# Two transformer layers on one core: late query projections split between two memories, epsilon on GpSimd, and a planner that books transfers and a slow clock

## The chip, the cores and the metric

One core of one Trainium2 chip. The time is that of the device in microseconds for one execution, from first to last instruction and what lies around them; lower is better. The engines are TensorE (PE in the profile; its weight loads are PEld), VectorE (DVE), ScalarE (ACT), GpSimd (POOL) and SyncE (SP), which issues nearly all transfers. Scores, projections and attention sums are made by TensorE in PSUM, in banks of 512 float32 columns.

## The reference

Two layers, each an attention part and a dense part with a squared ReLU, over 2048 tokens of 448 features; 16 heads of 28 features, 1792 hidden features, one set of weights for both layers, bfloat16.

```python
def _A_ref(x, wqkv, wo):
    H = 16; Dh = D // H
    q, k, v = ...
    p = _softmax(jnp.einsum("bhqd,bhkd->bhqk", q, k) * Dh ** -0.5, axis=-1)
    o = jnp.einsum("bhqk,bhkd->bhqd", p, v)
    return ... @ wo
def _B_ref(x, w1, b1, w2, b2):
    h = jnp.maximum(x @ w1 + b1, 0)
    return (h * h) @ w2 + b2
x = A_x
for layer in range(2):
    x = x + _A_ref(_layernorm(x), A_wqkv, A_wo)
    x = x + _B_ref(_layernorm(x), B_w1, B_b1, B_w2, B_b2)
return x
```

The layer norm is (x - mean) / sqrt(variance + 1e-5) over the features.

## The kernel before

**Work.** Tokens stand in 16 tiles of 128. Heads stand in four groups g of four, each head in a band of 32 rows or columns. Queries go in blocks of 256 (the last two of layer 1 in blocks of 128). For a layer, a query block and a group of heads there is a pass: over all keys, scores are made (`sc`, L1326), exponentials taken (`pt`), and the products with the values summed in one bank (`oT`, L1516). A unit is 512 columns of scores, one bank; there are 2048 units.

**Exponentials on two engines.** A turn of `s_stream` makes three or four units. ScalarE takes two or three banks with one instruction (L1369). The remaining unit, if `apart` allows it, goes to VectorE: a taking (L1389) writes a piecewise linear power of two as int16, two shifted copies follow (L1405, on GpSimd or VectorE, whichever the planner finds sooner), and VectorE adds one of the copies to the first line (L1418). Memory that is dead at the time serves for them, in cells of 512 columns that `cells` lists: nine of its own (`v_c`), and parts of the keys and values of the layer that isn't running, of `K_sb[0]` among them.

**Rows after attention.** VectorE copies or adds the sums out of PSUM (L1539, L1541). The softmax sums stand in one row of each band; `norm_pair` sends them through transfers: spread out (`dn`), inverted by VectorE (L1621), written to DRAM (`scr`) and brought back to all rows of a band (`rec`), then multiplied (L1640). For the last blocks `norm_turn` inverts them on VectorE alone, with two transposes and no transfer (L1582 to L1598). `chain` then makes the output projection, the layer norm, the hidden layer with ReLU (L1720) and square (L1727), the second matrix, and in layer 0 the next layer's projections of the block (`qkv`).

**Layer norm.** VectorE takes mean and variance (L672, L677), adds epsilon (L700), GpSimd raises to the power -1/2 (L697, `rstd`), VectorE normalizes (L796).

**Late queries.** In layer 0, while block qb runs, layer 1's normalized input of blocks 4 to 7 is stored in `Q_sb` at the block's own columns, since its queries can only be written when layer 0's are dead. The projections for these blocks (`late_queries`) are then made in two halves, of two groups each. Both read all of the stored input and write over it; so the copy of the first half waits, through the token `qq`, until the matmuls of the second are done.

**Beside other work.** A projection of K = 4 x 128 rows leaves its last 128 rows to guests: `visit` makes it in bands of 32 rows beside score matmuls that use other bands (L927); what found no place is made whole at the end (`fin`, L870). Score matmuls are repeated as filler, and junk matmuls (`heat`) made, where the recent load of TensorE is low.

**The order.** The program is built by `Planner.run`: generators offer operations, each with an engine, a booked duration and what it depends on; the planner picks the one that can start first (with priorities) and issues it, so each engine's row is fixed beforehand. Its numbers are set again and again while it runs: `PACE` maps the count of exponentials so far to values for the names of the rules, and `FORCE` and `SKIP` name turns in which a unit must or mustn't go to VectorE. Transfers are an engine of the planner too, "DMA": `dur` is the time for which a transfer keeps that engine, `lat` what passes after it until the data is there.

Of the kernel before, what the change touches and what calls it, by code (L numbers as in the profile page):

```python
# [29 lines left out]
def lines(x, by):  # L30
# [138 lines left out]
GNEXT = 0.5  # L169
BEHIND = 3  # L170
# [9 lines left out]
         'GUEST': 1, 'GUEST1': 0, 'GUESTB': 1, 'STEER': 1, 'GWAIT': 1, 'GOPEN': 0.8},  # L180
    8: {'EV': 3.5, 'FORCE': (15,)},
    16: {'LOW': 0.5, 'SKIP': (18,)},
    24: {'EPRIO': 6, 'MARGIN': 3, 'FORCE': (29,)},
    32: {'ASIDE': 0, 'V_PRIO': 3},
    40: {'RES2': 4},
    48: {'HOLD': 5, 'SKIP': (49,)},
    56: {'EV': 2.9},
    64: {'MMC': 0.46, 'SKIP': (71,)},
    72: {'TASIDE2': -0.2, 'V_LAST': 2.5},
    80: {'MMC': 0.3, 'LEAD': 6, 'GNEXT': 0.3},  # L190
    88: {'MMC': 0.46, 'BUSY': 0.95, 'PRE': 1.2},
    104: {'TB2': 2.4, 'SOON': 1},
    120: {'LAG': 12, 'V_PRIO': 6},
    128: {'TASIDE2': -0.4, 'GOPEN': 2, 'SPAN': 15},
    144: {'MORE': 1, 'ASIDE': 0.2, 'FORCE': (148,)},
    160: {'HEAT': 0.45, 'V_LATE': 4.6},
    168: {'PORTP': 0.1, 'SKIP': (171,)},
    176: {'PNEAR': 0.35, 'FORCE': (181,)},
    192: {'V_AGE': 8, 'SKIP': (198,)},
    224: {'MFREE': 1, 'GIDLE': 0.1, 'FORCE': (226,)},  # L200
    256: {'V_PAST': 3},
    264: {'C_PRIO': 2.6, 'V_PRIO': 3, 'SKIP': (271,)},
    272: {'LADD': 0.1, 'BEHIND': 0, 'PMAX': 6},
    280: {'NEAR_U': 6},
    288: {'LAG': 1, 'SOON': 1.5, 'C_PRIO': 2.1, 'SKIP': (295,)},
    296: {'GIDLE': 0.5},
    312: {'V_PRIO': 6},
    320: {'BUSY': 1.0},
    328: {'EPRIO': 4, 'GIDLE': 0.1, 'SKIP': (332,)},
    336: {'PLIM': 4, 'LADD': 0.3},  # L210
    344: {'PORTP': 0.3, 'SKIP': (348,)},
    360: {'V_AGE': 6, 'PORTP': 2, 'C_PRIO': 1.6},
    368: {'LADD': 0.05, 'FORCE': (369,)},
    384: {'PORTP': 0.3},
    392: {'MFREE': 5, 'KEEP': 3, 'PWAIT': 1.5, 'SKIP': (393,)},
    408: {'SOON': 0.3, 'FORCE': (413,)},
    416: {'SPARE': 0},
    432: {'SPARE': 3, 'PORTP': 2, 'SKIP': (439,)},
    440: {'LAG': 16},
    448: {'URGE': 8, 'ASIDE': 2},  # L220
    456: {'PRE': 0.3},
    464: {'LADD': 0, 'PWAIT': 0.6},
    472: {'V_AGE': 8, 'SKIP': (479,)},
    480: {'V_WAIT': 8},
    488: {'LAG': 3},
    496: {'BUSY': 1.05, 'CHUNK': 2},
    512: {'PWAIT': 0.1, 'V_PAST': 1},
    520: {'RES': 1},
    536: {'TB2': 1.6, 'FAR': 9, 'MORE': 3, 'FORCE': (537,)},
    544: {'V_WAIT': 3, 'NEAR_U': 0},  # L230
    560: {'RES2': 2, 'SKIP': (563,)},
    568: {'RES': 4},
    576: {'EV': 3.5, 'SKIP': (583,)},
    584: {'LEAD': 2},
    592: {'SKIP': (599,)},
    600: {'PWAIT': 0.3},
    608: {'HEAT': 0.3},
    616: {'HEAT': 0.45, 'V_LAST': 3},
    624: {'VGAP': 0.08},
    632: {'BEHIND': 3, 'URGE': 3, 'BUSY': 1.0},  # L240
    640: {'MFREE': 1},
    648: {'V_PAST': 2, 'SKIP': (649,)},
    656: {'V_LAST': 2.2, 'PRE': 0, 'SKIP': (658,)},
# [36 lines left out]
class Planner:  # L280
# [3 lines left out]
    def __init__(self):  # L284
# [11 lines left out]
        self.seen = []  # L296

# [43 lines left out]
    def run(self):  # L341
        while self.streams:
# [88 lines left out]
def kernel(  # L431
# [77 lines left out]
    def flat_of(t):  # L509
        return t[:, :, :].rearrange("p g s -> p (g s)")  # L510
# [1321 lines left out]
```

## Time and profile before

| | |
|---|---|
| median of 3 runs (802.45 to 804.76) | 804.6 us |
| the profiled execution | 803.5 us |
| its span, first to last instruction | 801.7 us |
| first exponential starts, last one ends | 9.16 us, 786.60 us |
| mean granted TensorE clock | 0.994 |
| moved by transfers | 18.12 MB, mean 23 GB/s |

The page of a profile gives for each engine its busy time and its share of the span. A table of stages gives the same for stretches of the span, and the granted clock in each. A line on a group of instructions names the line of the program, the engine, the operation, what is written from what, its shapes and count, then the busy time and the mean duration of one in ns, then the engine's idle time just before them and what ended most of it. A group's busy time is less than count times mean where neighbours on an engine overlap.

### The profile page before, as it was taken

What the parts mean: (1) busy time and instruction counts of PE and PEld (TensorE: products, weight loads), DVE (VectorE), ACT (ScalarE), POOL (GpSimd) and SP (SyncE); (2) the same over time, 40 slices, a digit from 0 to 9 for tenths busy, and PEclk for the clock granted to TensorE, in tenths of its full rate; (3) what the DMA queues carried; (4) which work ended last, traced back from release to release, by engine and by line L of the source; (5) the groups of instructions that cost most, each with busy time, mean ns of one, the idle gap of its engine ahead of it and who ended that gap; (6) DMA issues with size and microseconds to landing.
All of it is one profiled execution on the core that took longest, in us unless ns stands there. A gap on an engine that the chain in (4) does not pass through costs nothing.

```text
span 801.7 us, 29097 instructions
## 1 busy us (share of the span) xinstructions
PE 769.9 (96%) x12227; PEld 412.2 (51%) x12227; DVE 736.9 (92%) x1645; ACT 783.8 (98%) x701; POOL 439.9 (55%) x677
## 2 busy tenths in 40 slices
PE   9999988999999999999999999889999999999997
PEld 6455544555535455454545445435455455445665
DVE  8999998999999999999999999889999999999854
ACT  9999999999999999999999999999999999999994
POOL 3266664565675575465455566545666566675200
PEclk9999999999999999999999999989999999999999
DMA  9300011000000000000000000011000000000000
GB/s 248 87 3 2 3 30 30 16 17 16 7 12 16 16 17 16 16 3 16 2 2 3 2 2 3 6 38 32 23 21 22 27 22 23 21 18 13 21 21 13
DMA packets 32479, 18.12 MB, mean 23 GB/s; under 512 B 17818, under 2 KB 31899, under 8 KB 32348
## 3 DMA queue, kind: packets, MB, share of 16 engines
q1 hardware_dynamic: 32204, 16.16, 7.3%
q8 instruction: 95, 1.56, 0.8%
q14 instruction: 36, 0.29, 0.1%
q10 hardware_dynamic: 144, 0.11, 0.0%
HBM read 13.98 MB, written 2.06 MB: 20 GB/s over the span
## 4 chain that ended last, share of the span: by engine, by line
PE 65%; ACT 18%; DVE 11%; issue 5%; DMA 2%; POOL 0%; ACTq 0%; SPq 0%; DVEq 0%
PE mt L851 27%; PE sc L1326 18%; ACT pt L1369 18%; PE oT L1516 14%; PE mt L927 2%; DVE pt L1389 2%; PE tp L736 1%; PE sc L851 1%; DVE st L672 1%; DVE x_sb L1649 1%; DVE v_c L1389 1%; DMA scr<-dn 1%; DVE xn L796 1%; DVE Q_sb L945 1%; PE mt L870 1%
## 5 line engine op out<-in xcount | busy, mean ns | idle before, releaser
L1369 ACT ACTIVATE pt<-sc 128x1536 bf16<-128x1536 f32 (+1 forms) x683 | 771.9, 1285 | 5.6 <-PE sc L1326 4.9
L1326 PE MATMUL sc<-Q_sb,K_sb 32*128 32x256 bf16 (+1 forms) x4562 | 277.4, 266 | 17.9 <-ACT pt L1369 14.6
L1516 PE MATMUL oT<-pt,V_sb 128*32 128x256 bf16 (+1 forms) x4062 | 191.0, 269 | 2.0 <-DVE Q_sb L945 0.8
L1326 PEld LDWEIGHTS <-K_sb 32*128 32x128 bf16 x4562 | 98.9, 92 | 167.1 <-issue 111.0
L1389 DVE TENSOR_SCALAR pt<-sc 128x512 int16<-128x512 f32 x207 | 141.0, 683 | 9.9 <-PE sc L1326 8.6
L1516 PEld LDWEIGHTS <-V_sb 128*32 128x32 bf16 x5074 | 117.2, 96 | 61.2 <-issue 56.3
L1405 POOL TENSOR_SCALAR v_c<-pt 128x512 int16<-128x512 int16 x160 | 107.5, 672 | 64.8 <-DVE pt L1389 27.3
L851 PE MATMUL mt<-xnT,w 128*128 128x256 bf16 (+1 forms) x912 | 120.6, 270 | 1.5 <-DVE r L1720 1.2
L1405 POOL TENSOR_SCALAR K_sb<-pt 128x512 int16<-128x512 int16 x114 | 75.7, 664 | 48.5 <-DVE pt L1389 23.5
L851 PEld LDWEIGHTS <-w 128*128 128x128 bf16 x952 | 78.4, 98 | 36.6 <-issue 28.1
L1720 DVE TENSOR_SCALAR r<-mt 128x512 bf16<-128x512 f32 x107 | 72.9, 683 | 7.4 <-PE mt L851 7.1
L1516 PE MATMUL oT<-v_c,V_sb 128*32 128x256 bf16 (+1 forms) x436 | 65.4, 276 | 1.9 <-DVE r L1720 1.4
L851 PE MATMUL mt<-w,V_sb 128*128 128x448 bf16 x274 | 65.3, 355 | 0.0
L697 POOL TENSOR_TENSOR rstd<-mv,mhalf 128x2 f32<-128x2 f32 (+1 forms) x34 | 24.7, 727 | 65.1 <-DVE mv L700 46.2
L1405 POOL TENSOR_SCALAR V_sb<-pt 128x512 int16<-128x512 int16 x66 | 42.9, 650 | 24.9 <-DVE pt L1389 11.7
L1418 DVE TENSOR_TENSOR pt<-pt,v_c 128x512 bf16<-128x512 bf16 x96 | 41.2, 435 | 2.4 <-POOL v_c L1405 2.0
L1405 POOL TENSOR_SCALAR v_c<-v_c 128x512 int16<-128x512 int16 x47 | 31.0, 660 | 21.4 <-DVE v_c L1389 12.4
L1516 PE MATMUL oT<-K_sb,V_sb 128*32 128x256 bf16 (+1 forms) x304 | 42.4, 269 | 0.1
L1649 DVE TENSOR_TENSOR x_sb<-x_sb,mt 128x448 bf16<-128x448 bf16 x61 | 37.1, 610 | 3.1 <-PE mt L851 2.6
L672 DVE BATCH_NORM_STATS2 st<-x_sb 128x6 f32<-128x448 bf16 x63 | 38.6, 614 | 0.5 <-DMA x_sb<-in_A_x_dram 0.4
L1389 DVE TENSOR_SCALAR v_c<-sc 128x512 int16<-128x512 f32 x55 | 37.5, 681 | 1.5 <-PE sc L1326 1.4
L1405 POOL TENSOR_SCALAR V_sb<-V_sb 128x512 int16<-128x512 int16 x40 | 26.5, 662 | 21.2 <-DVE V_sb L1389 10.4
(172 smaller groups left out, 1031.7 us busy)
## 6 DMA issues: line engine op xcount, KB each, us to landing
rec<-scr SPq DMA_DIRECT2D x54, 128.0 KB
out_dram<-x_sb SPq DMA_DIRECT2D x15, 112.0 KB
x_sb<-in_A_x_dram SPq DMA_DIRECT2D x7, 224.0 KB
w<-in_B_w_dram SPq DMA_DIRECT2D x1, 1568.0 KB
w<-in_B_w_dram SPq DMA_DIRECT2D x1, 1344.0 KB
dn<-oT_sb SPq DMA_DIRECT2D x54, 4.0 KB
V_sb<-in_A_wqkv_dram SPq DMA_DIRECT2D x4, 168.0 KB
scr<-dn SPq DMA_DIRECT2D x27, 8.0 KB
```

The source lines that it names most:

```text
L672: nc.vector.bn_stats(out=box["st"][:, :], in_=x_sb[:, t0 + j, :] if src is None else src())
L697: nc.gpsimd.tensor_tensor(out=rstd[:, a:b], in0=mv[0][:, a:b, 1], in1=mhalf[:, a:b], op=ALU.pow)
L851: nc.tensor.matmul(box["t"][:, c0:c0 + n], lhsT=lhsT() if callable(lhsT) else lhsT, rhs=rhs, start=a and "x" not in rest, stop=b or stop is m)
L927: t = nc.tensor.matmul(rest["box"]["t"][:, c0:c0 + n], lhsT=lhsT[rows], rhs=rhs[rows], start=start and j == 0, stop=stop and j == len(rest ...
L1326: nc.tensor.matmul(dst[k][:, i * nt * P:(i + 1) * nt * P], lhsT=K_sb[l][rows, g, (kb + i) * P:(kb + i + 1) * P], rhs=Q_sb[rows, g, t0 * P: ...
L1369: t = nc.scalar.activation(out=pt[:, 0:n], in_=gbuf[gi]["sc"][:, 0:n], func=AF.Exp, scale=float(np.log(2.0)) * 2.0 ** -FRAC)
L1389: t = nc.vector.tensor_scalar(out=z.bitcast(DT.int16), in0=src, scalar1=EXP_BASE, scalar2=0.0, op0=ALU.add, op1=ALU.max)
L1405: (nc.vector if e == "DVE" else nc.gpsimd).tensor_scalar(out=box[k].bitcast(DT.int16), in0=gbuf[gi]["z"].bitcast(DT.int16), scalar1=1.0, s ...
L1418: nc.vector.tensor_tensor(out=z, in0=z, in1=box[1], op=ALU.add)
L1516: nc.tensor.matmul(box["t"][DHP * hh:DHP * hh + DHP, 0:n], lhsT=V_sb[l][:, tb, 4 * g + hh, :], rhs=p, start=hh in starts and j == begins[h ...
L1649: nc.vector.tensor_tensor(out=x_sb[:, tb, lo:hi], in0=x_sb[:, tb, lo:hi] if src is None else src[:, lo:hi], in1=t[:, 0:hi - lo], op=ALU.add)
L1720: nc.vector.tensor_scalar(out=r[:, 0:w], in0=t[:, 0:w], scalar1=0.0, scalar2=None, op0=ALU.max)
```

## The change

1. **Late queries.** The half with groups 0 and 1 is copied to dead memory of `K_sb[0]` (its first 2048 columns, 512 for each of the four blocks) and no longer to `Q_sb`; scores of these blocks and groups read their queries there (`queries_of`). The wait on `qq` is gone, and the late projections take guests' bands like others. The four cells of `K_sb[0]` that lay there are no longer offered to layer 1's products (`R_c[41:45]`).
2. **Sums.** `norm_turn` can serve a block of a pair, for the blocks in `QFAST`; `PACE` sets `QFAST` to `([1, 0],)`.
3. **Planner.** The transfer `rec` is booked for 0.9 + 2.5 us of the queue with 0.2 behind it, and no longer 0.9 with 2.7. When TensorE's load over 3.4 us falls under 0.36, its operations are booked at 1.5 times their length for 4 us.
4. **Epsilon** is added by GpSimd, except in the first blocks of layer 0 and in the last block.
5. **Guests** that found no place are made a band at a time, with a pause between, and no longer all at once.
6. **`PACE`** is another table. There are also new switches that stay off (`NOCL`, `CPOOL`).

```diff
+BACK = 2.5
+COLD = 0.36
+EPOOL = 1
+QFAST = ()
 PACE = {
     0: {...
-         'GUEST': 1, 'GUEST1': 0, 'GUESTB': 1, 'STEER': 1, 'GWAIT': 1, 'GOPEN': 0.8},
-    8: {'EV': 3.5, 'FORCE': (15,)},
...
+         'GUEST': 1, 'GUEST1': 0, 'GUESTB': 1, 'STEER': 1, 'GWAIT': 1, 'GOPEN': 0.8, 'QFAST': ([1, 0],),
+         'CPOOL': 0, 'CASIDE': 0.3, 'HEAT': 0.6, 'WINDOW': 3.4},
+    8: {'NEAR': 6, 'GUEST': 0, 'C_PRIO': 2.6},
+    16: {'PRE': 0, 'CHUNK': 3, 'PWAIT': 3},
...
+    56: {'PWAIT': 0.6, 'V_LATE': 6},
...
+            if e == "PE" and o.dur > 0.0 and s > 15.0 and not self.final:
+                if self.load(3.4) < COLD:
+                    self.cold = s + 4.0
+                if s < self.cold:
+                    o.dur *= 1.5
...
-                nc.vector.tensor_scalar(out=mv[0][:, a:b, 1], in0=mv[0][:, a:b, 1], scalar1=EPS, scalar2=None, op0=ALU.add)
-            ep = Op("DVE", 0.15, eps, deps=[mv[1][b - 1]])
+                (nc.vector if e == "DVE" else nc.gpsimd).tensor_scalar(out=mv[0][:, a:b, 1], in0=mv[0][:, a:b, 1], scalar1=EPS, scalar2=0.0, op0=ALU.add, op1=ALU.add)
+            ep = Op(*(("POOL", 0.25) if EPOOL and not early else ("DVE", 0.15)), eps, deps=[mv[1][b - 1]])
...
-        if rest["bands"]:
+        wait = last
+        while rest["bands"]:
 
             def fin(e):
...
-                while rest["bands"]:
+                else:
                     visit(rest, rest["bands"][0])
+                    rest["by"] = last
...
+            rest["fin"] = None
+            if rest["bands"]:
+                wait = Op("+", GNEXT, None, deps=[last])
+                yield wait
...
+            if away:
+                d = flat_of(K_sb[0])[:, 512 * (t0 // 2 - 4):512 * (t0 // 2 - 3)].rearrange("p (g q) -> p g q", g=2)
...
                 for a in qs:
-                    yield from turned(*a, after=[("qq", t0)])
-                yield Op("-", 0.0, None, deps=[last.deps[0]], sets=("qq", t0))
+                    yield from turned(*a, away=a[4] == 0)
...
-        out += R_c[41:45]
...
+    def queries_of(l, g, t0, nt):
+
+        if l == 1 and t0 // 2 >= QDEF and g < 2:
+            c = 512 * (t0 // 2 - 4) + 256 * g + t0 % 2 * P
+            return flat_of(K_sb[0])[:, c:c + nt * P]
+        return Q_sb[:, g, t0 * P:(t0 + nt) * P]
...
-                                         rhs=Q_sb[rows, g, t0 * P:(t0 + nt) * P],
+                                         rhs=queries_of(l, g, t0, nt)[rows],
...
-            if last:
+            if last and (l, qb) in QFAST:
+                pair["own"].need = 2
+                pl.spawn(3, norm_turn(l, qb, g, oe, pair, pair["own"]))
+            elif last:
...
-        r = Op("DMA", 0.9, back, deps=[d2], acq=R_rec, lat=2.7)
+        r = Op("DMA", 0.9 + BACK, back, deps=[d2], acq=R_rec, lat=2.7 - BACK)
```

Since the planner and its table change, nearly every row of every engine stands elsewhere. Counted in the two orders:

| | before | after |
|---|---|---|
| ScalarE, exponentials of three banks | 332 | 318 |
| ScalarE, exponentials of two banks | 351 | 365 |
| VectorE, takings of a bank, and as many adds | 350 | 364 |
| shifted copies on VectorE | 86 | 116 |
| shifted copies on GpSimd | 614 | 612 |
| epsilon additions of L700 on VectorE, on GpSimd | 33, 0 | 4, 29 |
| score matmuls, filler among them | 4562 | 4700 |
| guests' matmuls in a band of rows | 130 | 79 |
| their matmuls made whole at the end | 64 | 44 |
| matmuls of L851 (now L871), guests apart | 2069 | 2119 |
| junk matmuls | 15 | 27 |
| transposes in `norm_turn` | 24 | 24 |
| chains of transfers in `norm_pair` | 28 | 28 |

First place: VectorE's row where layer 1 begins, at the late projections. `Q_sb<-mt` (L945, now L972) is the copy of a half, `pt<-sc` a taking, `oT` rows the sums of a pass. Before, in the order of the row:

```order
L1389 TENSOR_SCALAR pt<-sc 128x512
L945 TENSOR_SCALAR Q_sb<-mt 128x2x256 x2
L1418 TENSOR_TENSOR pt<-pt,V_sb_105 128x512
L1418 TENSOR_TENSOR pt<-pt,K_sb_102 128x512
L1418 TENSOR_TENSOR pt<-pt,v_c 128x512
L1389 TENSOR_SCALAR pt<-sc 128x512
L945 TENSOR_SCALAR Q_sb<-mt 128x2x256
L1389 TENSOR_SCALAR pt<-sc 128x512
L945 TENSOR_SCALAR Q_sb<-mt 128x2x256
```

And now:

```order
L972 TENSOR_SCALAR K_sb_102<-mt 128x512
L1453 TENSOR_TENSOR pt<-pt,v_c 128x512
L1440 TENSOR_SCALAR h<-pt 128x512
L1453 TENSOR_TENSOR pt<-pt,h 128x512
L972 TENSOR_SCALAR Q_sb<-mt 128x2x256
L1578 COPY K_sb_102<-oT 128x256
L1580 TENSOR_TENSOR oT_sb<-oT,K_sb_102 128x256
L972 TENSOR_SCALAR K_sb_102<-mt 128x512
L1424 TENSOR_SCALAR v_c<-sc 128x512
```

Both halves of a block stood close together before; now the first half goes to `K_sb_102` (layer 0's keys) by itself, with other work between it and the second.

Second place: VectorE's row in the middle of layer 1, near the 590th exponential. `pt<-sc` and `v_c<-sc` are takings, L1405 (now L1440) shifted copies, L1418 (now L1453) the adds. Before:

```order
L1418 TENSOR_TENSOR v_c<-v_c,K_sb_102 128x512
L1389 TENSOR_SCALAR pt<-sc 128x512 x2
L1418 TENSOR_TENSOR pt<-pt,K_sb_102 128x512
L1389 TENSOR_SCALAR pt<-sc 128x512
L1405 TENSOR_SCALAR v_c<-pt 128x512
L1418 TENSOR_TENSOR pt<-pt,v_c 128x512
```

And now:

```order
L1440 TENSOR_SCALAR V_sb_105<-pt 128x512
L1440 TENSOR_SCALAR v_c<-pt 128x512
L1453 TENSOR_TENSOR pt<-pt,v_c 128x512
L1424 TENSOR_SCALAR pt<-sc 128x512
L1440 TENSOR_SCALAR K_sb_102<-pt 128x512
L1440 TENSOR_SCALAR h<-pt 128x512
L1424 TENSOR_SCALAR pt<-sc 128x512
L1453 TENSOR_TENSOR pt<-pt,h 128x512
```

Before, VectorE made one of the two copies of a taking here and GpSimd the others; now VectorE makes both, twice in a row.

Third place: GpSimd's row at a layer norm in layer 1. `rstd<-mv,mhalf` is the power, `mv<-mv` the addition of epsilon, the others are shifted copies. Before:

```order
L1405 TENSOR_SCALAR V_sb_105<-pt 128x512
L697 TENSOR_TENSOR rstd<-mv,mhalf 128x2
L1405 TENSOR_SCALAR h<-V_sb_105 128x512
L1405 TENSOR_SCALAR K_sb_102<-V_sb_105 128x512
L1405 TENSOR_SCALAR K_sb_102<-v_c 128x512 x2
```

And now:

```order
L1440 TENSOR_SCALAR v_c<-pt 128x512
L1440 TENSOR_SCALAR K_sb_102<-pt 128x512
L720 TENSOR_SCALAR mv<-mv 128x2
L717 TENSOR_TENSOR rstd<-mv,mhalf 128x2
L1440 TENSOR_SCALAR K_sb_102<-pt 128x512 x2
```

The addition has moved from VectorE to the place just ahead of the power.

More of the change, by code (lines that the diff above doesn't have):

```diff
@@ L871, in fin @@
                     rest["bands"].clear()
-                while rest["bands"]:
+                else:
                     visit(rest, rest["bands"][0])
-            last = rest["fin"] = Op("PE", 0.0, fin, deps=[last])
+                    rest["by"] = last
+                if not rest["bands"]:
+                    guests.remove(rest)
+            last = rest["fin"] = Op("PE", 0.0, fin, deps=[wait])
             last.defer = GWAIT0 if rest["whole"] else GWAIT
@@ L877, in mm_tile @@
             yield last
-        elif bands and rest["by"] is not last:
+            rest["fin"] = None
+            if rest["bands"]:
+                wait = Op("+", GNEXT, None, deps=[last])
+                yield wait
+        if bands and rest.get("by", last) is not last:
             last = Op("+", 0.0, None, deps=[last, rest["by"]])
@@ L898, in settle @@
         else:
-            f.durs, f.mode, f.defer = (n * len(rest["bands"]),), "row", GWAIT
+            f.durs, f.mode, f.defer = (n,), "row", GWAIT
         f.dur = f.durs[0]
@@ L1427, in a_rest @@
         yield h
+        if apart_:
+            return
         yield o
@@ L1578, in norm_turn @@
         halves = lambda a: a.rearrange("p (b k) -> p b k", k=DHP)
+        sums = lambda: pass_box["t"][:, 0:n] if own is None else pass_box["t"][:, g % 2, 0:n]
         def turn(e):
             box["t"] = rp.tile([P, 2, QR], DT.float32, name="rec")
-            nc.vector.transpose(out=box["t"][:, 0, 0:n], in_=pass_box["t"][:, 0:n])
-        t = Op("DVE", 0.178 + n / 960, turn, deps=[oe], acq=R_rec)
+            nc.vector.transpose(out=box["t"][:, 0, 0:n], in_=sums())
+        t = Op("DVE", 0.178 + n / 960, turn, deps=[oe], acq=R_rec, port=own is not None)
         yield t
```

166 lines of the change are left out of this document (88 added, 78 removed).

## The prediction

> **What bounds the kernel now.** I read the page's totals first, then a table of stages, then the groups of instructions, the waits and short windows where a stage looked loose.
>
> ```profile
> span 801.7 us, 29097 instructions
> PE 769.9 (96%) x12227; PEld 412.2 (51%) x12227; DVE 736.9 (92%) x1645; ACT 783.8 (98%) x701; POOL 439.9 (55%) x677
> PE 65%; ACT 18%; DVE 11%; issue 5%; DMA 2%; POOL 0%; ACTq 0%; SPq 0%; DVEq 0%
> ```
>
> Three engines are nearly full. The chain of waits (third row) runs mostly along TensorE, but it takes the engine's in-order queue as it stands; which engine has no spare time is seen by stage. Columns below: the stretch, its length, then busy time and count of PE, PEld, DVE, ACT, POOL, then granted clock, DMA share, GB/s.
>
> ```profile
> 20.00:100.00 80.00, 77.03 (x1197) 40.88 (x1195) 77.17 (x172) 79.75 (x71) 44.85 (x69) 1.00 0.09 24
> 100.00:140.00 40.00, 34.52 (x560) 19.51 (x554) 35.15 (x75) 38.09 (x34) 22.78 (x34) 1.00 0.11 30
> 140.00:500.00 360.00, 353.34 (x5460) 183.69 (x5455) 343.69 (x750) 359.50 (x322) 212.28 (x332) 1.00 0.04 10
> 500.00:560.00 60.00, 53.70 (x796) 26.78 (x797) 51.98 (x118) 57.73 (x53) 32.09 (x50) 0.91 0.10 26
> 560.00:740.00 180.00, 176.85 (x2734) 90.17 (x2731) 172.88 (x379) 179.98 (x164) 112.28 (x167) 1.00 0.07 21
> 740.00:786.00 46.00, 43.94 (x1173) 29.06 (x1171) 32.26 (x82) 46.00 (x37) 7.84 (x12) 1.00 0.07 19
> ```
>
> ScalarE is never out of work from 140 to 500 and from 560 to 786: it is the bound there. Two stretches are loose on every engine, 100 to 140 (ScalarE idle 1.91 us) and 500 to 560 (2.27 us, clock 0.91). VectorE follows close behind: 94% from 20 to 560 (sum 507.99 of 540), 96% from 560 to 740.
>
> **ScalarE's work.** It takes exponentials of two or three banks of 512 scores.
>
> ```profile
> L1369 ACT ACTIVATE pt<-sc 128x1536 bf16<-128x1536 f32 x332 | 480.5, 1503 | 2.4 <-PE sc L1326 1.8
> L1369 ACT ACTIVATE pt<-sc 128x1024 bf16<-128x1024 f32 x351 | 358.5, 1078 | 3.2 <-PE sc L1326 3.1
> ```
>
> Neighbours overlap, so the means are no prices, but their difference is: 1503 - 1078 = 425 ns for a bank. From 560 to 740 the 164 exponentials are 70 wide and 94 narrow, which gives (179.98 - 70 x 0.425) / 164 = 0.916 us for a narrow one and 1.341 for a wide one. (From 140 to 500, 150 wide and 172 narrow, the same prices give 358.7 of the 359.5 seen.) All 683 cost 766.7 us. The new order has 318 wide and 365 narrow: 760.8. **ScalarE loses 14 banks, 5.95 us**; the 14 go to VectorE. By the order's tile numbers 8 of them lie before the 483rd exponential, 5 between the 483rd and the 646th (the stretch 560 to 740), 1 behind. The nine outside are worth 9 x 0.425 = 3.8 us where VectorE has room. It has it there: ahead of the 483rd it gets 7 more takings, 8 adds and 11 shifted copies, and loses 19 epsilon additions, some 7 us at the prices below, against 32 us idle between 20 and 560. **Term 1: -3.8.**
>
> **VectorE in layer 1.** This is where the change could pay back. Prices:
>
> ```profile
> L1389 DVE TENSOR_SCALAR pt<-sc 128x512 int16<-128x512 f32 x207 | 141.0, 683 | 9.9 <-PE sc L1326 8.6
> L1418 DVE TENSOR_TENSOR pt<-pt,v_c 128x512 bf16<-128x512 bf16 x96 | 41.2, 435 | 2.4 <-POOL v_c L1405 2.0
> L700 DVE TENSOR_SCALAR mv<-mv x33: 153/162/584, 4.0 to 770.1; 128x2 f32<-128x2 f32 x30, 128x1 f32<-128x1 f32 x3
> L1405 DVE TENSOR_SCALAR K_sb<-pt x21: 275/290/708, 139.2 to 751.2; 128x512 int16<-128x512 int16 x21
> L1405 DVE TENSOR_SCALAR v_c<-v_c x5: 285/684/707, 268.3 to 526.9; 128x512 int16<-128x512 int16 x5
> 560.00:740.00 180.00, 9.99 (x23) 108.55 (x162) 1.00 0.07 21
> 601.93 0.41 DVE L1727 TENSOR_TENSOR V_sb<-r 128x512 bf16<-128x512 bf16 x1
> 602.27 0.68 DVE L1389 TENSOR_SCALAR v_c<-sc 128x512 int16<-128x512 f32 x1
> 602.87 0.68 DVE L1720 TENSOR_SCALAR r<-mt 128x512 bf16<-128x512 f32 x1
> ```
>
> The last three rows are neighbours: a 0.68 instruction starts its successor 0.60 later, a 0.41 one 0.34 later, so 0.08 of each duration is overlap. A taking occupies 0.60, an add 0.36, an epsilon addition about 0.1. A shifted copy (L1405) has no single price: min/median/max run from 275 over 290 to 708 ns, and one row's median is 684. Its mean in this stage is 9.99 / 23 = 0.43 (sixth row: VectorE's, then GpSimd's copies). So it occupies 0.21 at the median, 0.35 at the mean, 0.61 at the long end.
>
> Between the 483rd and 646th exponential the new order gives VectorE 5 more takings (3.0), 3 adds (1.1), 5 fewer epsilons (-0.6), +0.1 net from a few norm and relu instructions that fall on the other side of the cut, and **44 shifted copies instead of 23**: 21 x 0.21 = 4.4, or 7.4, or 12.8. Together +8.0, +11.0 or +16.4 on 172.88: 180.9, 183.9 or 189.3 us, while ScalarE's own work falls to 177.9. So VectorE becomes the engine that ends last in this stage, and the stage changes by +0.9, +3.9 or +9.3; if work can slide over the stage's edges it could still fall by ScalarE's 2.1. VectorE can be full: its idle 7 us in this stage lie mostly before takings, waiting for scores (8.6 of the 9.9 us in the first row are such waits), and these vanish once it is late. I take **term 2: +1.0**, by the median, since most rows of shifted copies (K_sb, v_c, h, V_sb from pt) have it near 290.
>
> [...]
>
> **The loose stretches.** Rows: waits from 100 to 142, then windows of 2 us (columns as above).
>
> ```profile
> DVE oTn L1640 <- DMA rec<-scr: 2.4, 2, 1.6
> DVE dn L1621 <- DMA dn<-oT_sb: 1.4, 1, 1.4
> ACT pt L1369 <- PE sc L1326: 2.0, 4, 1.1
> 508.00:510.00 2.00, 1.60 (x32) 0.77 (x31) 0.42 (x1) 2.00 (x2) 0.00 (x0) 1.00 0.03 8
> 510.00:512.00 2.00, 1.47 (x18) 0.81 (x15) 0.85 (x2) 2.00 (x3) 0.00 (x0) 1.00 0.03 2
> 526.00:528.00 2.00, 1.94 (x28) 1.04 (x31) 1.97 (x7) 1.87 (x2) 0.92 (x2) 0.50 0.27 92
> 528.00:530.00 2.00, 2.00 (x23) 0.49 (x15) 0.85 (x3) 0.90 (x2) 1.17 (x3) 0.50 0.07 14
> 542.00:544.00 2.00, 1.95 (x21) 1.20 (x19) 1.69 (x4) 1.61 (x3) 1.84 (x3) 0.50 0.04 6
> ```
>
> From 100 to 140 VectorE stands at transfers of softmax sums (rec, dn), takings behind it are late, so TensorE gets no bank and ScalarE no scores. The planner had booked the returning transfer 0.9 us on the queue; it now books 3.4, so two of them no longer overlap in the plan, and multiplications stand later in VectorE's row. At the layer boundary VectorE and GpSimd run dry at 508, where each late query projection held both matmul banks; the clock then falls to 0.50 and ScalarE starves at 528 and 542. Now the first half of each projection is copied out at once (to K_sb0), and the filler is set by a higher load. At most 1.91 + 2.27 = 4.2 us can come back; nothing may, and a stall of the same size may appear elsewhere (+4.2). I take half: **term 3: -2.0.**
>
> [...]
>
> **TensorE.** 51 fewer matmuls of one row band stand beside scores, 30 more whole ones stand in the open, and 138 more score matmuls are repeated as filler.
>
> ```profile
> L851 PE MATMUL mt<-xnT,w 128*128 128x256 bf16 (+1 forms) x912 | 120.6, 270 | 1.5 <-DVE r L1720 1.2
> L1326 PE MATMUL sc<-Q_sb,K_sb 32*128 32x256 bf16 (+1 forms) x4562 | 277.4, 266 | 17.9 <-ACT pt L1369 14.6
> L851 PE MATMUL mt<-w,V_sb 128*128 128x448 bf16 x274 | 65.3, 355 | 0.0
> ```
>
> By busy time over count: 18 narrow ones at 0.132 and 12 wide ones at 0.238 are 5.2 us, the filler 138 x 0.061 = 8.4. On the path this is +13.6; hidden, 0. TensorE was 98% busy from 140 to 500 while ScalarE lost 0.5 us, and 14.6 of its 17.9 us before scores were waits for ScalarE, so most is hidden: **term 4: +1.0.**
>
> **At nothing.** Epsilon on GpSimd: no such instruction is in the trace; between VectorE's 0.16 and the 0.70 median of the power that follows it (L697). GpSimd is 55% busy and covers it; uncovered, 28 x 0.70 = 20 us of norm latency, against which only 1.1 us of waiting for rstd is seen:
>
> ```profile
> L697 POOL TENSOR_TENSOR rstd<-mv,mhalf x34: 554/698/870, 4.2 to 790.1; 128x2 f32<-128x2 f32 x30, 128x1 f32<-128x1 f32 x4
>   DVE xn L796: 1.1, 2
> ```
>
> Behind it on GpSimd stand shifted copies, for which adds wait; they have slack as long as the engine is half idle. The four cells lost in K_sb0 cost a wait only if none is free; layer 1's row of takings grew all the same. **The first rows' sums are not inverted by VectorE at all**: QFAST holds the list [1, 0] and the test looks for the tuple (1, 0), which no list equals, so both orders have 12 + 12 transposes and 28 transfer chains. That part does nothing.
>
> **Sum**: -3.8 + 1.0 - 2.0 + 1.0 = -3.8. The profiled execution took 803.5 us (span 801.7 and 1.8 around it); the three runs' median is 804.6. Against the middle of both, 804.05: **800.3 us**, its own range 797 to 803.5.
>
> **Rivals.** (a) Everything fits, as the loose edges and the vanishing waits for scores allow: stage -2.1, both stalls gone: -3.8 - 2.1 - 4.2 = -10.1, 794. Against it: VectorE at 180.9 or more in a stage of 177.9. (b) Slower: VectorE's added copies collide with GpSimd's in layer 1. With long copies +9.3 - 3.8 + 1.0 = +6.5, 810.5; with the mean price +1.1, 805. It decides from a copy of 0.38 us if the stalls stay, 0.48 if they shrink by 2; the mean was 0.43, the median 0.29, so it is near. For it: 21 more copies and GpSimd 62% busy there. Against it: the majority at 290 and a longer time for which the plan lets them take turns (PWAIT 0.6 there, 0.1 to 0.3 before). (c) The stalls move rather than go, the tight VectorE making new ones of about 4 us: 804.
>
> **Numbers.** Forecast 0.40, (a) 0.22, (b) 0.24, (c) 0.14. A measurement tells 0.3%, 2.4 us, from no change: faster means below 802.2 (0.36 of the forecast, all of (a): 0.58), slower above 807.0 (0.19 of (b), 0.02 of (c): 0.21), the rest 0.21. The range takes half of (a) and most of (b): 793 to 809.
>
> **What would show it.** ScalarE's exponentials at 425 ns a bank and 760.8 in all; idle in ScalarE's row between 560 and 740 ended by scores, with VectorE above 98% there (term 2) or not (a); the L1405 line on VectorE (now L1440) with 116 copies, mean 0.29 to 0.35 (forecast) or above 0.45 (b); no wait for rec and no clock under 0.9 (term 3). The forecast is wrong if VectorE is not the last engine in layer 1 or if new stalls of several us stand in layer 0.

## The result, and the profile after

| | before | after |
|---|---|---|
| median of 8 runs each | 804.5 us (801.0 to 805.21) | 799.55 us (799.07 to 800.87) |
| the profiled execution | 803.5 us | 799.5 us |
| its span | 801.7 us | 797.7 us |
| first exponential starts | 9.16 us | 9.58 us |
| last exponential ends | 786.60 us | 779.93 us |

The ratio is 0.9948, with a 95% interval from 0.9933 to 0.9963: faster by more than the 0.3% that can be told from no change. The forecast was 800.3.

The time of the kernel before goes with the clock that it was granted. Of its 80 executions beside the experiments below, the four with a mean clock of 1.000 took 801.3 to 801.9 us, and the 33 with 0.994, which the profiled one had too, took 803.5 to 805.6. The changed kernel's eight executions all had 0.999 or 1.000. So of the 4.95 us some 2 are left where the clocks are equal, and some 3 stand with the clock that fell at the layer boundary before and no longer does.

The page's totals of the changed kernel, in the order TensorE, its weight loads, VectorE, ScalarE, GpSimd, and its chain of waits by engine:

```profile
span 797.7 us, 29438 instructions
...
PE 775.0 (97%) x12386; PEld 418.1 (52%) x12386; DVE 731.9 (92%) x1673; ACT 779.7 (98%) x702; POOL 443.9 (56%) x704
...
PE 60%; DVE 17%; ACT 14%; issue 6%; DMA 1%; POOL 1%; ACTq 0%; SPq 0%; DVEq 0%; POOLq 0%
```

VectorE executes 28 more instructions than before and is busy 5.0 us less. The table of stages of the changed kernel (columns as in the prediction):

```profile
20.00:100.00 80.00, 78.81 (x1202) 41.67 (x1201) 76.38 (x173) 79.57 (x71) 45.57 (x72) 1.00 0.08 23
100.00:140.00 40.00, 37.38 (x593) 21.27 (x590) 37.27 (x79) 39.47 (x36) 26.18 (x40) 1.00 0.11 30
140.00:500.00 360.00, 353.36 (x5527) 183.51 (x5525) 336.14 (x748) 358.95 (x323) 218.00 (x352) 1.00 0.04 10
500.00:560.00 60.00, 56.43 (x884) 30.05 (x887) 55.60 (x129) 60.00 (x55) 32.46 (x49) 1.00 0.10 26
560.00:740.00 180.00, 177.61 (x2920) 92.62 (x2916) 177.84 (x412) 179.60 (x166) 106.94 (x165) 1.00 0.07 21
740.00:786.00 46.00, 44.31 (x1010) 28.74 (x999) 29.13 (x76) 41.30 (x34) 8.31 (x13) 1.00 0.07 18
```

ScalarE's idle time (length less busy time) falls from 1.91 to 0.53 us in 100 to 140 and from 2.27 to 0.00 in 500 to 560, where the clock is now 1.00. It rises from 0.50 to 1.05 in 140 to 500 and from 0.02 to 0.40 in 560 to 740. VectorE is 98.8% busy in the last of these, and yet ScalarE is not short of scores there.

ScalarE's groups of the changed kernel in 560 to 740, by shape (busy time, mean in ns, idle before):

```profile
L1403 ACT ACTIVATE pt<-sc 128x1024 bf16<-128x1024 f32 x101 | 101.3, 1061 | 0.3
L1403 ACT ACTIVATE pt<-sc 128x1536 bf16<-128x1536 f32 x65 | 95.3, 1489 | 0.1
```

At the prediction's prices, 0.916 and 1.341 us, these are 101 x 0.916 + 65 x 1.341 = 179.7 us, and 179.60 are seen: the price of a bank holds. Five banks fewer left room for two more exponentials in the same 180 us.

Shifted copies of the changed kernel, on VectorE and on GpSimd, in two stretches (busy time and count):

```profile
20.00:560.00 540.00, 18.18 (x68) 298.17 (x452) 1.00 0.06 15
560.00:740.00 180.00, 11.65 (x46) 101.80 (x155) 1.00 0.07 21
```

46 copies on VectorE cost 11.65 us in the second stretch, 0.25 each, where 23 cost 9.99 before, 0.43 each. Busy time counts the overlap of two copies in a row only once; by their durations the mean falls there from 0.445 to 0.284 us, and over the whole kernel from 0.434 to 0.289. So it isn't only that the added ones are short: the old ones became short as well. The two largest groups of the changed kernel (minimum, median, maximum in ns):

```profile
L1440 DVE TENSOR_SCALAR v_c<-pt x55: 230/286/706, 170.3 to 736.6; 128x512 int16<-128x512 int16 x55
L1440 DVE TENSOR_SCALAR K_sb<-pt x24: 261/286/293, 161.8 to 744.1; 128x512 int16<-128x512 int16 x24
```

Before, 31 of 86 copies took more than 0.45 us; now one of 116 does.

VectorE's wait for the returning sums, from the changed kernel's waits in 100 to 142 (total, times, longest), and windows of 2 us at the layer boundary:

```profile
DVE oTn L1683 <- DMA rec<-scr: 0.8, 2, 0.5
```

```profile
508.00:510.00 2.00, 2.00 (x30) 1.13 (x29) 1.12 (x3) 2.00 (x2) 0.00 (x0) 1.00 0.03 8
510.00:512.00 2.00, 1.94 (x38) 0.87 (x32) 2.00 (x5) 2.00 (x3) 0.74 (x2) 1.00 0.03 2
...
528.00:530.00 2.00, 1.35 (x28) 0.60 (x25) 1.97 (x6) 2.00 (x3) 1.13 (x2) 1.00 0.16 33
```

Both waits for transfers have shrunk (rec from 2.4 to 0.8, dn from 1.4 to none), and VectorE no longer runs dry at 510 (2.00 of 2 us; 0.85 before).

The end of ScalarE's row in the changed kernel (start, length, instruction, count, and in brackets the idle time before it and what ended it):

```profile
752.03 27.90 ACT L1403 ACTIVATE pt<-sc 128x1536 bf16<-128x1536 f32 x21 [0.31 <-PE sc L1360]
783.98 0.60 ACT L1761 ACTIVATE r<-mt 128x512 bf16<-128x512 f32 x1 [4.05 <-PE mt L871]
```

**The span's account.** The first exponential starts 0.4 us later (among the runs below that change nothing so early, it starts between 9.26 and 9.47, so part of this is the execution). From there to the end of the last one (752.03 + 27.90 = 779.93) pass 770.35 us and no longer 777.4. Of these 7.1, 5.95 are exponentials not made (760.8 for 766.7) and 1.15 is lost time that went away (9.55 for 10.7). But 17.8 us lie behind the last exponential and no longer 15.1: 2.7 more. Together +0.4 - 7.1 + 2.7 = -4.0, the difference of the spans. The medians differ by 4.95, which has the two profiled executions' places among their runs in it.

### The profile page after: what moved, and what is told of

It is laid out like the page before. It is cut to its first block, busy times and chain, and to the rows that moved or that the text cites. A ratio compares the mean times of both kernels' runs of the same rounds, so it can differ in the third digit from the quotient of the medians.

```text
span 797.7 us, 29438 instructions
## 1 busy us (share of the span) xinstructions
PE 775.0 (97%) x12386; PEld 418.1 (52%) x12386; DVE 731.9 (92%) x1673; ACT 779.7 (98%) x702; POOL 443.9 (56%) x704
## 4 chain that ended last, share of the span: by engine, by line
PE 60%; DVE 17%; ACT 14%; issue 6%; DMA 1%; POOL 1%; ACTq 0%; SPq 0%; DVEq 0%; POOLq 0%
PE mt L871 26%; PE sc L1360 18%; ACT pt L1403 14%; PE oT L1555 13%; DVE pt L1424 5%; DVE pt L1453 2%; DVE r L1763 2%; PE mt L954 1%; PE tp L756 1%; DVE st L692 1%; PE sc L871 1%; DVE V_sb L1770 1%; DVE x_sb L1692 1%; DVE xn L816 1%; PE mt L890 1%
## 5 line engine op out<-in xcount | busy, mean ns | idle before, releaser
L1360 PE MATMUL sc<-Q_sb,K_sb 32*128 32x256 bf16 (+1 forms) x4018 | 249.3, 268 | 12.2 <-ACT pt L1403 8.6
L1440 POOL TENSOR_SCALAR v_c<-pt 128x512 int16<-128x512 int16 x233 | 153.2, 658 | 96.6 <-DVE pt L1424 40.0
L1424 DVE TENSOR_SCALAR pt<-sc 128x512 int16<-128x512 f32 x277 | 188.7, 684 | 11.3 <-PE sc L1360 9.1
L1555 PE MATMUL oT<-pt,V_sb 128*32 128x256 bf16 (+1 forms) x4168 | 184.7, 268 | 0.4
L871 PE MATMUL mt<-xnT,w 128*128 128x256 bf16 (+1 forms) x904 | 120.7, 269 | 1.9 <-DVE xnT L768 1.0
L1440 POOL TENSOR_SCALAR K_sb<-pt 128x512 int16<-128x512 int16 x117 | 76.9, 657 | 60.2 <-DVE pt L1424 29.9
L871 PEld LDWEIGHTS <-w 128*128 128x128 bf16 x936 | 75.9, 97 | 37.7 <-issue 29.9
L1440 POOL TENSOR_SCALAR V_sb<-pt 128x512 int16<-128x512 int16 x86 | 56.3, 654 | 32.5 <-DVE pt L1424 14.5
L1453 DVE TENSOR_TENSOR pt<-pt,v_c 128x512 bf16<-128x512 bf16 x146 | 62.6, 437 | 2.2 <-POOL v_c L1440 1.8
L871 PE MATMUL mt<-w,V_sb 128*128 128x448 bf16 (+1 forms) x274 | 64.2, 350 | 0.0
L1440 POOL TENSOR_SCALAR v_c<-v_c 128x512 int16<-128x512 int16 x39 | 26.0, 668 | 25.3 <-DVE v_c L1424 13.9
L1360 PE MATMUL sc<-K_sb,K_sb 32*128 32x256 bf16 (+1 forms) x682 | 37.2, 250 | 0.7 <-ACT pt L1403 0.5
L871 PEld LDWEIGHTS <-V_sb 128*128 128x128 bf16 x302 | 23.4, 97 | 25.1 <-issue 11.6
L1555 PE MATMUL oT<-V_sb,V_sb 128*32 128x256 bf16 (+1 forms) x228 | 35.2, 273 | 0.1
```

The costliest lines, as they stand in the source:

```text
L871: nc.tensor.matmul(box["t"][:, c0:c0 + n], lhsT=lhsT() if callable(lhsT) else lhsT, rhs=rhs, start=a and "x" not in rest, stop=b or stop is m)
L1360: nc.tensor.matmul(dst[k][:, i * nt * P:(i + 1) * nt * P], lhsT=K_sb[l][rows, g, (kb + i) * P:(kb + i + 1) * P], rhs=queries_of(l, g, t0, ...
L1424: t = nc.vector.tensor_scalar(out=z.bitcast(DT.int16), in0=src, scalar1=EXP_BASE, scalar2=0.0, op0=ALU.add, op1=ALU.max)
L1440: (nc.vector if e == "DVE" else nc.gpsimd).tensor_scalar(out=box[k].bitcast(DT.int16), in0=gbuf[gi]["z"].bitcast(DT.int16), scalar1=1.0, s ...
L1453: (nc.vector if e == "DVE" else nc.gpsimd).tensor_tensor(out=z, in0=z, in1=box[1], op=ALU.add)
L1555: nc.tensor.matmul(box["t"][DHP * hh:DHP * hh + DHP, 0:n], lhsT=V_sb[l][:, tb, 4 * g + hh, :], rhs=p, start=hh in starts and j == begins[h ...
```

## The experiments

Times are medians, effects are against the changed kernel's 799.55, ratios against the kernel before, which ran beside each (its medians: 804.7 to 805.1). Instructions that are added as load write where nothing reads; nothing of the kernel is left out. They stand in the finished order: every other instruction keeps its place.

**Is ScalarE the bound in layer 0?** Twelve small exponentials more, in the changed kernel:

```diff
+                if gi in range(200, 440, 20):
+                    nc.scalar.activation(out=more[0].bitcast(DT.bfloat16)[:, 0:448], in_=b2w[:, :], func=AF.Exp)
```

> The changed kernel with every row in its place, and 12 more exponentials of 448 columns on ScalarE among its turns 200 to 420 (layer 0), whose results nothing reads; about 0.43 us each by the spacing of its neighbours, 5 us in all. Theory (ScalarE is the bound in layer 0): the time rises by about 5, to 804.5; before over this 1.000. Rival (TensorE or VectorE set the pace as much): it rises by 2.5 or less.

Measured: 804.09 us, +4.5, for 5.2 us of work (ratio 0.9992, interval 0.9984 to 1.0001).

**And in layer 1?** The same with `range(490, 646, 13)`, written to another tile that nothing reads by then.

> The same 12 exponentials among the turns 490 to 633 (layer 1). Theory (ScalarE is still the bound there, VectorE just fits): again about +5. Rival (the prediction's term 2, VectorE sets the pace of layer 1 and ScalarE waits): +2 or less, since they fall into ScalarE's idle time.

Measured: 804.01 us, +4.5, for 4.5 us of work (0.9997, 0.9985 to 1.0009). The middle of layer 1 in this run:

```profile
560.00:740.00 180.00, 174.82 (x2773) 91.17 (x2765) 174.68 (x402) 180.00 (x173) 104.34 (x161) 1.00 0.07 20
```

ScalarE is full, and VectorE has gone back to 97%. ScalarE is still a bound in both layers: what it does more comes out at the end, whole in layer 1 and nearly whole in layer 0.

**Has VectorE room in layer 0?** Twelve statistics instructions more on VectorE, each behind a taking:

```diff
+    extra = list(range(200, 440, 20))
...
+            if extra and gi >= extra[0]:
+                extra.pop(0)
+                nc.vector.bn_stats(out=idle6[:, :], in_=b2w[:, :])
```

> The changed kernel with every row in its place, and 12 more statistics of 448 columns on VectorE right behind takings between turns 200 and 420 (layer 0), whose results nothing reads; 0.61 us each, 0.53 by spacing, 6.4 us in all. Theory (VectorE, 93% busy there, has room): +0 to +1.5. Rival (VectorE's in-order row is on the path everywhere): +5 to +6.

Measured: 803.68 us, +4.1, for 5.6 us of work (0.998, 0.9971 to 0.999). The expectation missed. The twelve stand from 243.9 to 487.9 us. The two stretches in which they lie, in this run:

```profile
220.00:440.00 220.00, 214.37 (x3342) 112.28 (x3342) 205.00 (x447) 218.53 (x194) 132.16 (x214) 1.00 0.04 11
440.00:500.00 60.00, 57.78 (x914) 28.91 (x915) 56.85 (x133) 57.95 (x54) 33.63 (x56) 0.97 0.01 2
```

The same stretches of the changed kernel:

```profile
220.00:440.00 220.00, 215.67 (x3367) 112.88 (x3369) 201.96 (x441) 219.52 (x195) 132.81 (x216) 1.00 0.04 11
440.00:500.00 60.00, 58.78 (x954) 30.30 (x946) 58.34 (x135) 59.81 (x57) 35.49 (x59) 1.00 0.01 2
```

VectorE was only 92% busy from 220 to 440 and is 93% busy with the load, and still ScalarE stands idle 1.47 us there (0.48 without). From 440 to 500 it stands idle 2.05 us (0.19 without), 1.60 of them in one wait at 491, behind the last of the twelve, and the clock falls to 0.97. Not every execution loses the clock: the four of twelve with a mean clock of 1.000 took 801.99 to 802.53 us, +2.4 to +3.0, and the others 802.96 to 804.38. So about half of the load comes out where the clock holds, and the rest comes with the clock. A busy share under 100% was spare time in part only.

**And in layer 1?** The same load with `range(490, 646, 13)`.

> The same 12 statistics between turns 490 and 633 (layer 1), where VectorE is busy for 177.84 of 180 us. Theory (VectorE just fits, 2.2 us are left): +3 to +6, clearly more than in layer 0. Rival (there is still room): +1.5 or less.

Measured: 803.91 us, +4.4, for 4.8 us of work (0.9987, 0.9978 to 0.9995). The stage in this run, then ScalarE's waits in it (total, times, longest):

```profile
560.00:740.00 180.00, 174.08 (x2785) 89.88 (x2785) 178.78 (x415) 177.25 (x162) 103.73 (x160) 1.00 0.07 21
```

```profile
ACT pt L1404 <- PE sc L1361: 1.9, 7, 0.4
```

ScalarE falls to 177.25 us and now waits for scores, seven times up to 0.4 us. The number is as the theory had it. By the medians it isn't larger than in layer 0; but all eleven executions had a clock of 0.999 or 1.000 here, and beside the +2.4 to +3.0 of layer 0 at that clock it is. So layer 1 has less room than layer 0, as the prediction said, but layer 0 has far less than the prediction took.

**And in the kernel before?** The same load there, at the same exponentials.

> The kernel before with every row in its place and 12 more statistics on VectorE between turns 490 and 633 (layer 1), where it is busy for 172.88 of 180 us; 6.4 us by spacing. Theory (VectorE had 7 us to spare there): +0 to +2.5, less than in the changed kernel. Rival (its in-order row was on the path before too): +4 or more.

Measured: 807.1 us beside 805.07 without the load: +2.0 by the medians and +2.7 by the ratio, for 4.9 us of work (1.0033, 1.0015 to 1.0051).

```profile
560.00:740.00 180.00, 175.56 (x2698) 89.41 (x2693) 175.83 (x385) 178.60 (x162) 111.75 (x165) 1.00 0.08 21
```

VectorE has 175.83 us of work here and ScalarE falls to 178.60. Before the change VectorE had a margin in layer 1 of some half of the load; after it the load counts nearly whole. The change used that margin up.

**Do turns keep the copies short?** The planner makes some of GpSimd's instructions, the shifted copies among them, wait for the VectorE instruction that stands ahead of them in its plan, so that the two begin in turn (`PWAIT` says how long it lets one wait for that). The wait is taken out, and the order kept:

```diff
-                    self.tc.add_manual_dep(self.seen[0], self.guard.made[0].name,
-                                           mybir.DependencyInfo(mybir.DependencyClass.Sync, mybir.DependencyReason.DATA),
-                                           reason="turns at the port")
+                    pass
```

> The changed kernel with every row in its place, without the waits by which a GpSimd operation starts only after a given VectorE operation, for which no data calls. Theory (the turns keep the shifted copies on VectorE at 0.29 us each): their mean rises above 0.40, VectorE's busy time by 8 us or more, and the time by 2 to 6. Rival (the order of the rows alone keeps them apart): the mean stays below 0.32 and the time within 1 us of 799.5.

Measured: 844.23 us, **+44.7** (1.0499, 1.0472 to 1.0525), far beyond both expectations. The page's totals of this run:

```profile
PE 784.5 (93%) x12386; PEld 419.1 (50%) x12386; DVE 786.5 (93%) x1673; ACT 793.1 (94%) x702; POOL 450.2 (53%) x704
```

The same 1673 instructions keep VectorE busy for 786.5 us and not 731.9. Two groups of VectorE, an add and the normalization, in this run (busy time, mean ns, idle before):

```profile
L1451 DVE TENSOR_TENSOR pt<-pt,v_c 128x512 bf16<-128x512 bf16 x146 | 76.0, 529 | 0.6 <-POOL v_c L1438 0.2
...
L814 DVE TENSOR_SCALAR xn<-x_sb,mv,rstd 128x448 bf16<-128x448 bf16 x64 | 33.3, 544 | 2.8 <-POOL rstd L715 2.8
```

And in the changed kernel:

```profile
L1453 DVE TENSOR_TENSOR pt<-pt,v_c 128x512 bf16<-128x512 bf16 x146 | 62.6, 437 | 2.2 <-POOL v_c L1440 1.8
...
L816 DVE TENSOR_SCALAR xn<-x_sb,mv,rstd 128x448 bf16<-128x448 bf16 x64 | 24.2, 402 | 2.6 <-POOL rstd L717 2.5
```

An add grows from 437 to 529 ns in the mean, a normalization from 402 to 544. Shifted copies of this run (VectorE's, GpSimd's):

```profile
20.00:560.00 540.00, 23.95 (x66) 291.03 (x435) 0.99 0.05 13
560.00:740.00 180.00, 13.66 (x41) 92.93 (x140) 1.00 0.08 23
```

The copies grow to 0.36 and 0.33 us by busy time (0.38 in the mean of their durations), less than the 0.40 expected, so the adds and the rest pay more than the copies do. In the trace of the kernel before, 51 of VectorE's 86 shifted copies start while a GpSimd instruction is under way: they take 537 ns in the mean, and all 31 that take more than 0.45 us are among them and end 0.15 us behind that instruction; the other 35 take 295 ns at most. In the changed kernel 11 of 116 start so, with a mean of 326 ns. Still, 0.36 is less than the 0.43 of the kernel before, which has turns: where the copies stand in the row counts too. What part of the step from 0.43 to 0.25 belongs to the longer `PWAIT` was not tried by itself; the runs with code and table apart, below, show that it comes with the table.

**Epsilon back on VectorE**, with everything else in place:

```diff
-                (nc.vector if e == "DVE" else nc.gpsimd).tensor_scalar(out=mv[0][:, a:b, 1], in0=mv[0][:, a:b, 1], scalar1=EPS, scalar2=0.0, op0=ALU.add, op1=ALU.add)
+                nc.vector.tensor_scalar(out=mv[0][:, a:b, 1], in0=mv[0][:, a:b, 1], scalar1=EPS, scalar2=None, op0=ALU.add)
```

> The changed kernel with every other row in its place; the 28 epsilon additions of pairs and the last single one stand on VectorE again, at the place where the plan has them. VectorE gets some 3 to 5 us more work, GpSimd loses about 7. Theory (the move helps a little, where VectorE is full): +0 to +2 us. Rival (it frees GpSimd's place on the norm's path and costs nothing): 0, within 0.5.

Measured: 801.15 us, +1.6 by medians and +0.8 by the ratios (0.9958, 0.9943 to 0.9973; the interval overlaps the changed kernel's). VectorE is busy 2.0 us more in all (733.9). This part is worth some 0.8 to 1.6 us. On GpSimd the addition takes 272 ns at the median, and the power behind it is no longer than before (minimum, median, maximum; changed kernel):

```profile
L720 POOL TENSOR_SCALAR mv<-mv x29: 222/272/726, 16.2 to 759.7; 128x2 f32<-128x2 f32 x28, 128x1 f32<-128x1 f32 x1
...
L717 POOL TENSOR_TENSOR rstd<-mv,mhalf x34: 557/699/747, 4.4 to 783.6; 128x2 f32<-128x2 f32 x30, 128x1 f32<-128x1 f32 x4
```

**The booking of the returning transfer undone:**

```diff
-BACK = 2.5
+BACK = 0.0
```

> The changed kernel with the returning transfer booked as before (0.9 us of the queue, 2.7 behind it); the rows of all engines are the same up to about the 460th exponential, and planned anew behind it; ScalarE's work comes to 761.2, 0.4 more. The prediction gave the end of the stall at 100 to 140 to the booking; then ScalarE's idle time there would be back at 1.9. With the same rows it should stay at 0.5. At the boundary, 500 to 560: idle of 1 to 2 us again if the booking removed it, 0 to 0.5 if not. Time 800 to 802.

Measured: 810.33 us, +10.8 (1.0074, 1.0047 to 1.01). Missed. The order changes only from about the 460th exponential on. Stages of this run:

```profile
100.00:140.00 40.00, 37.36 (x596) 21.17 (x594) 37.19 (x79) 39.45 (x36) 26.25 (x40) 1.00 0.11 30
...
500.00:560.00 60.00, 53.54 (x830) 28.59 (x830) 52.53 (x121) 56.32 (x52) 32.29 (x50) 0.97 0.10 25
560.00:740.00 180.00, 175.65 (x2777) 90.32 (x2780) 172.83 (x405) 178.69 (x163) 95.95 (x150) 1.00 0.08 21
```

The stall from 100 to 140 stays away without the booking (0.55 us idle), so the booking did not end it; the table orders that stretch alike with both. The stall at the boundary is back (3.68 us, clock 0.97), so this one order without the booking stalls there. Whether the booking itself keeps the stall away, or only the order that the table was made for, one replanned order can't tell. The other side of that boundary, the booking for a slow clock, needs no run: planned without that rule, the program is the same row for row on every engine.

**The first rows' sums inverted by VectorE in fact**, by the tuple that the test looks for:

```diff
-'QFAST': ([1, 0],)
+'QFAST': ((1, 0),)
```

> The changed kernel with QFAST as a tuple, so that the first block of layer 1 has its sums inverted by VectorE: 8 transposes more (some 3.5 us), two chains of transfers fewer; the rows are the same up to about the 460th exponential and planned anew behind it; ScalarE's work 761.2. Theory (that part is dead in the change and small when live): 799.5 to 801.5. Rival (it would have been worth something): under 798.5.

Measured: 807.34 us, +7.8 (1.004, 1.0024 to 1.0055). Missed: worse than expected.

```profile
500.00:560.00 60.00, 55.69 (x866) 29.75 (x865) 56.72 (x133) 60.00 (x54) 33.19 (x52) 1.00 0.06 16
560.00:740.00 180.00, 173.70 (x2798) 89.68 (x2799) 173.78 (x407) 176.25 (x162) 98.42 (x152) 1.00 0.08 21
```

The boundary itself stays full; the loss is in what stands behind it, which is planned anew: ScalarE is idle 3.75 us from 560 to 740, and 21.1 us remain behind its last exponential, 3.3 more than in the changed kernel. The dead part cost nothing. That it would not have helped is shown for this table alone, which was made for another order.

**Code and table apart.** All code of the change with the old `PACE`, then the old code with the new `PACE`:

> All code of the change with the table of numbers of before. The orders give ScalarE 354 wide and 329 narrow exponentials, 776.1 us by the prices of the prediction, 9.4 more than before. Theory (the gain comes from how many banks the table gives to VectorE, and ScalarE is the bound): 804.5 + 9.4 = 814, less what the code saves in the loose stretches (up to 4). Rival (the code saves by itself): 804.5 or less.

> The code of before with the new table (names that it doesn't know are ignored). ScalarE has 345 wide and 338 narrow ones, 772.3 us, 5.6 more than before. Theory: 810, plus up to 5 for loose stretches, which the table was not made for here. Rival (the table alone holds the gain): 800.

Measured: 823.2 us (1.0236, 1.021 to 1.0261) and 839.48 us (1.0435, 1.0407 to 1.0462); expected were 814 and 810, so both are slower than the theories said. Stages of the first, then of the second:

```profile
20.00:100.00 80.00, 73.82 (x1154) 39.47 (x1153) 74.76 (x164) 72.27 (x64) 43.27 (x68) 1.00 0.07 22
...
560.00:740.00 180.00, 176.66 (x2727) 91.49 (x2727) 169.40 (x363) 180.00 (x162) 103.59 (x156) 1.00 0.08 23
```

```profile
20.00:100.00 80.00, 78.11 (x1149) 43.25 (x1147) 74.75 (x172) 71.52 (x63) 38.02 (x58) 1.00 0.08 22
...
560.00:740.00 180.00, 168.84 (x2596) 88.72 (x2594) 156.44 (x363) 174.24 (x154) 77.84 (x119) 0.98 0.08 23
```

Each half alone is slower than the kernel before, by 19 and 35 us; both lose 7.7 and 8.5 us of ScalarE from 20 to 100 already. The table fits one order only, so the gain can't be split into a part of the code and a part of the table. The short copies can be: VectorE's shifted copies from 560 to 740 (then GpSimd's), in the first run and in the second:

```profile
560.00:740.00 180.00, 12.53 (x26) 98.63 (x146) 1.00 0.08 23
```

```profile
560.00:740.00 180.00, 10.64 (x41) 74.05 (x114) 0.98 0.08 23
```

With the old table they stay long under the new code (0.48 us each), and with the new table they are short under the old code (0.26). So the table makes them short, by its `PWAIT` or by the order that it gives.

**The end.** A larger `SLACK` from the 648th exponential, to have fewer matmuls left behind the last scores:

```diff
-    648: {'MMC': 0.9},
+    648: {'MMC': 0.9, 'SLACK': 1.2},
```

> The changed kernel with one more number in the table at turn 648 (SLACK 1.2: other work may delay a turn of scores by more); all rows are the same up to about the 650th exponential. ScalarE's work is the same, and the matmuls behind the last scores fall from 13.7 us of columns to 11.6 (before the change: 10.5). Theory (the 2.7 us by which the stretch behind the last exponential grew are the work left over there): 797 to 798.5. Rival (the longer end comes from somewhere else, or the delay moves it ahead of the last exponential): 799.5.

Measured: 803.95 us, +4.4 (0.999, 0.9978 to 1.0003). The end of ScalarE's row in this run:

```profile
777.06 6.39 ACT L1403 ACTIVATE pt<-sc 128x1536 bf16<-128x1536 f32 x5 [0.32 <-PE sc L1360]
784.66 0.60 ACT L1761 ACTIVATE r<-sc 128x512 bf16<-128x512 f32 x1 [1.21 <-PE sc L871]
```

In the orders, the matmuls behind the last scores fall from 13.7 to 11.6 us of columns (10.5 before the change). But the last exponential ends at 783.45, 3.5 us later, and 17.65 us remain behind it. The expected time was missed. The traces still show where the longer end comes from. TensorE's last stretch, from the end of the last layer norm's transposes to its last matmul, before, after and in this run:

```profile
792.36:798.97 6.61, 6.57 (x88) 5.79 (x86) 2.95 (x8) 2.06 (x4) 0.00 (x0) 1.00 0.05 19
```

```profile
785.35:794.54 9.19, 9.15 (x109) 7.37 (x106) 3.11 (x9) 3.51 (x7) 0.43 (x1) 1.00 0.08 23
```

```profile
789.39:797.50 8.11, 8.11 (x98) 6.82 (x96) 2.33 (x6) 2.07 (x4) 0.00 (x0) 1.00 0.01 3
```

It works nearly without a break in all three. The stretch is 2.6 us longer after the change and holds 21 matmuls more, and that is nearly all of the 2.7. The last block's own work is the same in both, which points to work left over from ahead of it. In this run the stretch is 1.1 us shorter again, but nearly as much was added ahead of it and behind it, and the last exponential came later. So clearing the work in this way costs more than it brings.

## Why the prediction came out right, step by step

- **What bounds.** Right for ScalarE (4.5 us of load cost 4.5 and 5.2 cost 4.5). Wrong in large part for VectorE in layer 0: "32 us idle between 20 and 560" was read as room, and 5.6 us of load there cost 4.1, or 2.4 to 3.0 where the clock held. The planner found places for its added takings; the finished order has less room for more than the idle time says.
- **Term 1, -3.8.** The price of a bank and the 760.8 us hold.
- **Term 2, +1.0.** It came out as -1.7: ScalarE's five banks fewer (-2.1), less 0.4 of new idle. (From the start of the 483rd to that of the 646th exponential the traces show 180.6 us before and 178.9 after.) The mis-sized part is the shifted copies. The prediction set 21 added copies at 0.21 on top of the old ones' time, +4.4 of its +8.0. The group went from 9.99 to 11.65, +1.7 for 23 more, since the old ones shortened too. With +1.7 the sum is 178.2; measured 177.84 from 560 to 740, which holds two exponentials more than before. So VectorE ends level with ScalarE and not behind it; the load runs show both at the limit. "The forecast is wrong if VectorE is not the last engine in layer 1", says the prediction: by that sign the mechanism of this term fell, though the time came out inside the range. One row was also read too widely: the 8.6 us of waits for scores are those of the whole kernel, and in this stage 3.4 of VectorE's 7.1 idle us were such waits. And at its own price of 0.1 the five epsilon additions are -0.5, not -0.6.
- **Term 3, -2.0.** It came out as -3.65: both stalls nearly gone (-1.38 and -2.27). Half was too little. And the reason given for the first was wrong: undoing the transfer's booking leaves that stretch as it is. For the second, one order planned without the booking has the stall again, the booking for a slow clock changes nothing in this plan, and no run puts the late queries back by themselves, so what keeps the boundary full stays open. At the boundary the clock is part of the gain: where the kernel before kept its clock it was some 3 us faster.
- **Term 4, +1.0.** TensorE is busy 5.1 us more, and ScalarE's idle time in the two full stages grew by 0.9 us in all; no more can be pinned on it. From 140 to 500, 144 wide and 179 narrow exponentials are 357.1 us at the prices and 358.95 are seen, where it was 358.7 and 359.50: 1.1 us more that shows as no idle. From start to start, 44 of these exponentials are followed more than 0.05 us later than their price, 5.2 us in sum; before it was 31 and 3.6. So it is small waits, most of them hidden in the overlap of neighbours. What made them late is open.
- **At nothing.** Epsilon on GpSimd is worth some 0.8 to 1.6 us rather than nothing; the dead `QFAST` is dead.
- **Not in the sum:** 2.7 us more behind the last exponential, 0.4 at the start (part of it the execution), 0.55 more idle from 140 to 500. The forecast did not look at the end of the row at all.

So terms 1 and 2 gave 2.7 us more than forecast and term 3 gave 1.65 more, and the end, the start and layer 0's losses took about as much back. The direction rests on what was argued, ScalarE's 5.95 us and the two stalls; that the total meets within 1 us rests on errors that cancel, which is luck.

Of the rivals, (a) was right on the stages (stage -1.7 of -2.1, stalls -3.65 of -4.2) and missed the end. (b) fell: the mean copy of the stage lasts 0.284 us, under its 0.38, and no run shows the long price for every added copy, which its +9.3 took: one of the 116 takes more than 0.45 us. That VectorE's instructions grow beside GpSimd's is measured: without turns an add takes 529 ns and not 437. (c) shows small, as 0.9 us of new idle from 140 to 500 and 560 to 740.

## What to carry to other kernels

An engine that is 92% busy may have far less spare time than its idle 8% when its instructions stand in a fixed order and hold score banks (here 2.4 to 3.0 us of a load of 5.6 came out at the end, and 3.4 to 4.8 where the clock fell with it): put a known load on it and see what comes out, before calling the idle 8% room. When instructions are added to a group whose durations run from 0.28 to 0.71 us, price the whole group anew and not only the added ones. Compare executions at the same granted clock before putting a difference down to the work. Read the end of the row, behind the last instruction of the bound engine, as a term of its own.

## What the runs showed of the hardware that was not expected

What VectorE and GpSimd cost each other when nothing makes them take turns: with the same instructions in the same order, only without turns, VectorE is busy 54.6 us more in all (731.9 to 786.5), GpSimd 6.3 us (443.9 to 450.2), and the kernel takes 44.7 us more. It falls on the two-input adds too (437 to 529 ns), and on the normalization (402 to 544 ns), and not on the copies alone.
